# Agent attention ahead of a feed-forward: key scores from two parts (bf16 and fp32r) instead of three, their fp32r products set among the feed-forward's, and the query exchanges made by transfers

## The chip, the core and the metric

The kernel runs on one core of a Trainium2 chip. The metric is the device time of one execution in microseconds; the span of the profile runs from the first to the last instruction of the program. Engines are named as in the profile: PE (TensorE, matmuls), PEld (its weight loads), DVE (VectorE), ACT (ScalarE), POOL (GpSimd) and SP (SyncE, which issues most loads and stores).

## The reference

Four batches of 12480 queries, keys and values of width 128 meet through 49 agents; the result, 49920 tokens of width 128, goes through a feed-forward of width 2048. All inputs are fp32.

```
scale = 1 / sqrt(128)
sm(a, b): softmax over the last axis of scale * (a @ b.T)
agent_v = sm(agents, k) @ v            # per batch, 49 x 128
x       = sm(q, agents) @ agent_v      # per batch, 12480 x 128
h = x.reshape(49920, 128) @ w_in       # 128 x 2048
out = (h * sigmoid(1.702 * h)) @ w_out # 2048 x 128
```

## The kernel before

The product agent_v @ w_in is formed once per batch, so that the first layer of the feed-forward takes the 49 attention weights of a token as its rows. The tokens are cut into 52 groups of 960 (13 per batch). A group is a **turn** of 17 **gaps**; in 16 of them PE does one **unit**, a slice of 128 of the 2048 hidden columns.

A unit on PE is nine pairs of matmuls of 480 columns. `up` makes three pairs into `ph` (high and low f16 parts of weights and attention, each half of the tokens on its own half of the array's rows); `down`, called twice in a gap, makes six pairs into `po` for a unit that is some six gaps older. Both matmuls of a pair use one half of the array's rows each and run side by side. ACT makes the gelu `g` from `ph`; `gh` and `gl`, high and low parts of `g`, are made by ACT or DVE (f16), or by a casting transfer that POOL issues and a subtraction on DVE (fp32r; which units go that way is in `MOVED`).

Between units, `gap(t)` calls the jobs planned for gap t: all the attention work of the later batches. The order of instructions on every engine is the order in which the code is written; nothing is rescheduled. Numbers such as `K_AT`, `MAX_AT`, `SUMS_AT` and `BACK_AT` say in which gap a job stands.

Key scores of the batches 1 to 3: the keys come in 13 groups of 960 per batch. 37 of these 39 groups are scored by `scores`, in two **runs** in neighbouring gaps t and t+1; the first two groups of batch 1 are done in plain fp32 (`scores_exact`). For a group, `split` cuts the fp32 keys `kt` into three bf16 parts. The first is the upper half of each word. DVE makes `rest` as `kt` minus that (line 241) and then the third part from `rest` (line 243), each for one half of the group, so four DVE instructions in the gaps t-4 to t-1. A run then has for each of four blocks of keys four pairs of bf16 products with the agents' parts in `ag_part`: 98, 98, 49 and 49 columns, from `kt`, `rest`, `kt` and `rest`. All 16 pairs of a run stand in one block ahead of the gap's unit.

Where a PSUM bank passes from one half of the array's rows to the other, `half_matmul` lets the new writer wait for a matmul noted by `rest()`, through an instruction on SP's queue (a relay). `rest()` is called at the start of a gap and after `up`.

Queries: scores of two groups lie transposed on DVE with the 49 agents of a token on two blocks of 32 partitions, so the largest value (`query_max`) and the sum (`query_sums`) of each block have to be exchanged with the neighbouring block. `exchange` does that with four copies of 32x30 on DVE (line 680), once for the largest values (`tops`, then `query_shift` at line 693) and once for the sums (then `query_recip` at line 712).

Of the kernel before, what the change touches and what calls it, by code (L numbers as in the profile page):

```python
# [8 lines left out]
F32 = mybir.dt.float32  # L9
# [9 lines left out]
P = 128  # L19
# [14 lines left out]
V_AT = ((0, 6, 12), (4, 11))  # L34
OWN_EXP = (12, 11)
MAX_AT = (21, 23, 25)
SUMS_AT = (3, 5)
BACK_AT = (6, 12)
HIGH_AT = (8, 14)
LOW_AT = (9, 14.5)  # L40
# [21 lines left out]
def kernel(  # L62
# [158 lines left out]
    for i in range(3):  # L221
        nc.vector.tensor_copy(out=ag_part[:, :, i, :], in_=rest)
        if i < 2:
            ag_rest = work.tile([P, B, A], F32, name="ag_rest", tag="o")
            nc.vector.tensor_sub(out=ag_rest, in0=rest, in1=ag_part[:, :, i, :])
            rest = ag_rest

    def halves(t):
        w = t.bitcast(BF16).rearrange("p (n w) -> p n w", w=2)
        return w[:, :, 1], w[:, :, 0]  # L230
# [1 line left out]


    def split(t):
        r = work.tile([P, GT + PAD], F32, name="rest", tag="rest", bufs=1)
        nc.gpsimd.memset(t[:, :PAD], 0.0)

        def piece(i):
            s = slice(0, CH + PAD) if i < 2 else slice(CH + PAD, GT + PAD)
            if i % 2 == 0:  # L240
                nc.vector.tensor_sub(out=r[:, s], in0=t[:, s], in1=halves(t)[0][:, s])
            else:
                nc.vector.tensor_sub(out=halves(r)[1][:, s], in0=r[:, s], in1=halves(r)[0][:, s])  # L243

        return (halves(t)[0], halves(r)[0], halves(r)[1]), piece

    writers = {}
    order = [0, None]
# [33 lines left out]
    def two_banks():  # L282
        return ps_m.tile([P, 2, 512], F32, name="ps_m")

    def scores(b, parts, ps, run, wide):


        x0, x1, x2 = parts
        if wide:
            products = [(x0, 0, 2, 0), (x1, 0, 2, 0), (x0, 2, 1, 0), (x2, 0, 1, 1)]  # L290
        else:
            products = [(x0, 0, 1, 0), (x0, 1, 1, 0), (x0, 2, 1, 0), (x1, 0, 1, 0), (x1, 1, 1, 0), (x2, 0, 1, 0)]
        for j in range(KB // 2):
            for i, (x, y, n, group) in enumerate(products):
                for c in range(2):
                    bank = c ^ run
                    t = (bank * KB // 2 + j) * TB
                    r = slice(c * H, (c + 1) * H)
                    at = (j * 2 + group if wide else j) * A
                    half_matmul(  # L300
                        (ps.name, bank),
                        c,
                        out=ps[:, bank, at : at + n * A],
                        lhsT=x[r, t : t + P],
                        rhs=ag_part[r, b, y : y + n, :].rearrange("p y a -> p (y a)"),
                        start=(run == 0 and i == 0 and j == 0),
                        stop=(run == 1 and i == len(products) - 1 and j == KB // 2 - 1),
                        skip_group_check=True,
                    )

    def scores_exact(b, x, out):

# [8 lines left out]
    def score_banks():  # L321
        ps = two_banks()
        return ps, ps[:, :, : KB // 2 * A].rearrange("p c (j a) -> p c j a", a=A)
# [352 lines left out]
    def exchange(t, x, quarters, by):  # L676

        for i in quarters:
            to = i ^ 1
            by(out=x[to * BL : (to + 1) * BL], in_=t[i * BL : (i + 1) * BL])  # L680

    def query_turn(n, ps):
        if n // 2 not in es:
            es[n // 2] = work.tile([P, 2, CH], F32, name="e")
        nc.vector.transpose(out=es[n // 2][:, n % 2, :], in_=ps[:, :CH])
# [55 lines left out]
    def up(f, wts, pairs, factor):  # L741
        wh, wl = wts
        q_hi, q_lo = pairs
        cols = slice(f * P, (f + 1) * P)
        ph = up_banks()
        products = [(wh, q_hi), (wh, q_lo), (wl, q_hi)]
        for k, (w, q) in enumerate(products):
            for c in range(2):
                r = slice(c * H, c * H + KR)
                half_matmul(  # L750
                    (ph.name, c),
                    c,
                    out=ph[:, c, :CH],
                    lhsT=w[r, cols],
                    rhs=q[r],
                    start=(k == 0),
                    stop=(k == 2),
                )
        g = gpool.tile([P, 2, CH], F32, name="g", bufs=G_BUFS)
        nc.scalar.activation(out=g, in_=ph[:, :, :CH], func=AF.Gelu_apprx_sigmoid, scale=factor)  # L760
        return g
# [53 lines left out]
    def down(u, gh, gl, po, swap, begin, end):  # L815
        products = down_products(u, gh, gl)
        for i, (w, x) in enumerate(products):
            for c in range(2):
                to = c ^ swap
                r = slice(c * H, (c + 1) * H)  # L820
                half_matmul(
                    po[to][0],
                    c,
                    out=po[to][1][:, :CH],
                    lhsT=w[r],
                    rhs=x[r, to, :],
                    start=(begin and i == 0),
                    stop=(end and i == len(products) - 1),
                )

    def down_whole(u, gh, gl, po, end):
        products = [(c, i) for c in range(2) for i in range(3)] if end else [(c, i) for i in range(3) for c in range(2)]
# [75 lines left out]

    def do_key_scores(b, g, c):
        if c == 0:  # L910
            banks[b, g] = wide_banks() if (b, g) in wide else score_banks()
        if (b, g) not in exact:
            scores(b, k_parts[b, g], banks[b, g][0], c, (b, g) in wide)
        elif c == 0:
            scores_exact(b, kts.pop((b, g)), columns(banks[b, g][0]))

# [335 lines left out]
    def plan_queries_of(k, alone):  # L1252
        t = LAG + (2 * k - 3) * GAPS
        d = BEHIND if 2 * k - 3 >= FREE else 0
        if k == 1:
            for at_, q in ((LAG + 3, 2), (LAG + 11, 3)):
                put(at_, lambda q=q: do_query_scores(q))
                put(at_ + 1, lambda q=q: do_query_turn(q))
            before = (LAG + 13, LAG + 14, LAG + 15)
        elif alone:  # L1260
            for i, at_ in enumerate((t - GAPS, t)):
                put(at_ - 12, lambda q=2 * k + i: do_query_load(q))
                put(at_, lambda q=2 * k + i: do_query_scores(q))
                put(at_ + 1, lambda q=2 * k + i: do_query_turn(q))
            before = tuple(t + x for x in MAX_AT)
        else:
            put(t - (12 if k > 2 else 4), lambda: do_query_load(2 * k))
            put(t - (9 if k > 2 else 3), lambda: do_second_load(2 * k + 1))
            put(t + d, lambda: do_query_pair(k))
            for i in range(2):  # L1270
                put(t + d + (0.5, 1)[i], lambda i=i: do_query_turn(2 * k + i))
            before = tuple(t + d + x for x in MAX_AT)
        put(before[0], lambda: do_query_max(k))
        put(before[2], lambda: do_query_shift(k))
        t = LAG + (2 * k - 1) * GAPS
        put(t, lambda: query_exp(k))
        put(t + SUMS_AT[0], lambda: do_query_sums(k))
        put(t + BACK_AT[0], lambda: do_query_recip(k))
        for i in range(2):
            quarters = (2 * i, 2 * i + 1)  # L1280
            put(before[1], lambda q=quarters: do_exchange(k, tops, q, nc.vector.tensor_copy))
            put(t + SUMS_AT[1], lambda q=quarters: do_exchange(k, sums, q, nc.vector.tensor_copy))
            put(t + BACK_AT[i], lambda i=i: do_query_back(k, i))
            put(t + HIGH_AT[i], lambda m=2 * k + i: do_query_high(m))
            put(t + LOW_AT[i], lambda m=2 * k + i: do_query_low(m))
# [171 lines left out]
    def gap(t):  # L1457
        n, k = divmod(t - LAG, GAPS)
        final = n == B * NG - 1
        if t < LAG:  # L1460
            u = t if t < LAG - 1 else None
        elif final:
            u = n * NF + LAG + k
        elif k == 0:
            u = LAG - 1 if n == 0 else None
        else:
            u = n * NF + LAG + k - 1
        before, late[:] = list(late), []
        rest()
        for job in at.pop(t, ()):  # L1470
            job()
        if u is not None:
            if u < total:
                do_up(u)
                rest()
            if k != NF:
                for i in low_of(u, n, k):
                    do_low(i)
        if t >= LAG:
            do_downs(n, k)  # L1480
        if u is not None and k == NF:
            for i in low_of(u, n, k):
                do_low(i)
        for job in at.pop(t + 0.5, ()):
            job()
        for u in before + soon:
            do_high(u)
        soon.clear()
        if k == 2 or final:
            send()  # L1490

    def do_downs(n, k):
# [7 lines left out]
        first_whole = NF - LAG - 1 if n == B * NG - 1 else NF  # L1500
        if 0 < k <= first_whole:
            do_down(n, k - 1, True)
        if k < first_whole:
            do_down(n, k, False)
        elif k < NF:
            do_down_whole(n, k)
        else:
            store(n, po.pop(n))
# [44 lines left out]
```

## Time and profile before

| | |
|---|---|
| median of three runs | 1816.1 us (1814.37 to 1817.16) |
| profiled execution, its own time | 1814.4 us |
| span of its profile | 1812.6 us |
| PE busy | 1772.2 us, 98% |
| DVE busy | 1662.7 us, 92% |
| ACT busy | 1558.2 us, 86% |
| POOL busy | 136.4 us, 8% |

The profiled execution took 1.8 us more than its span. Matmuls are pipelined and their recorded ends overlap, so what PE needs is read from the distance between starts. Idle time of an engine is put down to what released it.

### The profile page before, as it was taken

The numbers are of one execution on the slowest core, as the hardware profiler recorded it, in microseconds if no ns is written. First come the engines' busy times: TensorE is split into PE (matmuls) and PEld (weight loads), VectorE is DVE, ScalarE is ACT, GpSimd is POOL, SyncE is SP. The second block draws the span as 40 slices with busy tenths as digits, with TensorE's granted clock in tenths as the row PEclk, the third lists the DMA queues.
The fourth block names the chain that finished last, engine by engine and source line by source line (L and its number), as shares of the span: only waits on it lengthen the run. The fifth ranks groups of instructions, "written<-read, shape, count | busy, mean of one in ns | idle before, by whom it ended". The sixth has DMA issues, their size and how long they took to land. (4 is left out here: it accounts for less than half of the span.)

```text
span 1812.6 us, 45302 instructions
## 1 busy us (share of the span) xinstructions
PE 1772.2 (98%) x18905; PEld 1099.4 (61%) x18905; DVE 1662.7 (92%) x2337; ACT 1558.2 (86%) x1621; POOL 136.4 (8%) x312
## 2 busy tenths in 40 slices
PE   8899999999999999999999999999999999999999
PEld 8576666677565565566666666566655554555454
DVE  8889998999999999999989999999989889999996
ACT  4677899898878888998888988989878999999997
POOL 0111101111010100101100000011100000000000
PEclk9999999999999999999999999999999999999999
DMA  9565434555442442555443443455421011101000
GB/s 356 184 207 154 157 107 146 171 178 191 135 150 89 152 133 87 182 177 183 170 134 118 130 127 118 136 180 182 167 100 56 23 56 34 47 32 56 13 34 34
DMA packets 78494, 230.41 MB, mean 127 GB/s; under 512 B 8144, under 2 KB 28240, under 8 KB 78288
## 3 DMA queue, kind: packets, MB, share of 16 engines
q1 hardware_dynamic: 43728, 108.25, 19.4%
q0 software_dynamic: 34560, 119.26, 18.5%
q8 instruction: 148, 2.42, 0.6%
q14 instruction: 58, 0.48, 0.1%
HBM read 82.68 MB, written 25.56 MB: 60 GB/s over the span
## 5 line engine op out<-in xcount | busy, mean ns | idle before, releaser
L760 ACT ACTIVATE g<-ph,scales 128x960 f32<-128x960 f32 x832 | 869.5, 1053 | 180.5 <-PE ph L262 173.4
L262 PE MATMUL po<-gh,wo_half 64*128 64x480 f16 x4056 | 738.1, 363 | 6.3 <-DVE o L853 3.8
L262 PE MATMUL ph<-q_hi,wh 56*128 56x480 f16 x3328 | 656.2, 365 | 3.3 <-ACT g L760 3.1
L262 PEld LDWEIGHTS <-wo_half 64*128 64x128 f16 x7236 | 396.2, 94 | 357.8 <-issue 55.9
L801 DVE SCALAR_TENSOR_TENSOR gl<-g,scales,gh 128x960 f16<-128x960 f32 x500 | 592.4, 1208 | 8.0 <-ACT gh L786 6.8
L262 PE MATMUL po<-gl,wo_half 64*128 64x480 f16 x2028 | 411.5, 362 | 4.0 <-DVE gl L801 3.3
L262 PE MATMUL po<-gh,wo 64*128 64x480 f32 x1776 | 415.4, 450 | 0.0
L786 ACT ACTIVATE gh<-g,scales 128x960 f16<-128x960 f32 x361 | 395.6, 1096 | 11.5
L262 PEld LDWEIGHTS <-wh 56*128 56x128 f16 x4992 | 260.9, 94 | 225.5 <-issue 45.4
L262 PE MATMUL ph<-q_lo,wh 56*128 56x480 f16 x1664 | 334.1, 361 | 0.0
L804 DVE TENSOR_TENSOR gl<-g,gh 128x960 fp32r<-128x960 f32 x222 | 253.5, 1148 | 19.0 <-DMA gh<-g 15.6
L262 PEld LDWEIGHTS po<-gh,wo 64*128 64x128 f32 x1776 | 203.6, 185 | 35.5 <-issue 0.6
L792 POOL DMA_DIRECT2D gh<-g x201 | 107.7, 536 | 1501.3 <-ACT g L760 1476.5
L262 PE MATMUL po<-gl,wo 64*128 64x480 f32 x888 | 189.0, 379 | 1.0 <-DVE gl L804 1.0
L801 DVE SCALAR_TENSOR_TENSOR gl<-g,gains,gh 128x960 f16<-128x960 f32 x110 | 131.2, 1207 | 0.2
L262 PE MATMUL ps_m<-gh,wo_half 64*128 64x480 f16 x768 | 128.4, 362 | 0.0
L784 DVE TENSOR_SCALAR gh<-g,scales 128x960 f16<-128x960 f32 x139 | 98.9, 711 | 13.6 <-ACT g L760 13.6
L262 PEld LDWEIGHTS po<-gl,wo 64*128 64x128 f32 x888 | 103.0, 187 | 7.2 <-DVE gl L804 4.5
L786 ACT ACTIVATE gh<-g,gains 128x960 f16<-128x960 f32 x92 | 100.8, 1096 | 3.0
L262 PE MATMUL ps_m<-gl,wo_half 64*128 64x480 f16 x384 | 71.7, 361 | 0.0
L262 PE MATMUL ps_m<-ag_part,rest 64*128 64x49 bf16 (+1 forms) x1184 | 53.4, 192 | 9.4 <-DVE rest L243 9.4
L853 DVE TENSOR_SCALAR o<-po,backs 128x480 f32<-128x480 f32 x62 | 42.6, 714 | 20.6 <-PE po L262 20.0
(206 smaller groups left out, 1419.1 us busy)
## 6 DMA issues: line engine op xcount, KB each, us to landing
gh<-g POOLq DMA_DIRECT2D x201, 480.0 KB, 3.2
vt<-v SPq DMA_DIRECT2D x52, 512.0 KB, 4.2
kt<-kT SPq DMA_DIRECT2D x52, 480.0 KB, 4.2
outT<-o SPq DMA_DIRECT2D x104, 240.0 KB, 2.2
v_pair<-vt POOLq DMA_DIRECT2D x39, 512.0 KB, 3.7
qt<-qT SPq DMA_DIRECT2D x36, 480.0 KB, 3.8
e<-qT SPq DMA_DIRECT2D x14, 480.0 KB, 3.5
words<-w_in SPq DMA_DIRECT2D x4, 512.0 KB, 7.7
```

The source lines that it names most:

```text
L262: ins = nc.tensor.matmul(tile_position=(c * H, 0), **kw)
L760: nc.scalar.activation(out=g, in_=ph[:, :, :CH], func=AF.Gelu_apprx_sigmoid, scale=factor)
L784: nc.vector.tensor_scalar_mul(out=gh, in0=g, scalar1=by)
L786: nc.scalar.mul(out=gh, in_=g, mul=by)
L792: nc.gpsimd.dma_start(out=gh, in_=g)
L801: nc.vector.scalar_tensor_tensor(out=gl, in0=g, scalar=by, in1=gh, op0=ALU.mult, op1=ALU.subtract)
L804: nc.vector.tensor_sub(out=gl, in0=g, in1=gh.bitcast(F32))
L853: nc.vector.tensor_scalar_mul(out=o, in0=po[c][1][:, :CH], scalar1=back)
```

## The change

Keys are in two parts. The bf16 part is as before. The second is the whole remainder, written by one DVE subtraction per half group into a tile of type fp32r (now line 245, in the gaps t-3 and t-1). `ag_near` holds the agents in fp32r with a 50th column of zeros. A run keeps per block the two bf16 pairs from `kt` (98 and 49 columns); the two bf16 pairs from `rest` give way to one fp32r pair of 50 columns. This pair is not written there: it is put into the list `between`, and `fill()` takes one out after each pair of `up` and of `down`. `rest()` is called once more, behind the first `down` of a gap. In the diff, the two lines `fill()` stand at the end of the loops over pairs of `up` and `down`. `exchange_far` makes the exchanges by four transfers issued by POOL; the largest values of the second pair of groups (k = 1) and both exchanges of the first are still copies on DVE. `SUMS_AT[1]` goes from 5 to 4.

```
-            if i % 2 == 0:
+            if i % 2 == 1:
                 nc.vector.tensor_sub(out=r[:, s], in0=t[:, s], in1=halves(t)[0][:, s])
-            else:
-                nc.vector.tensor_sub(out=halves(r)[1][:, s], in0=r[:, s], in1=halves(r)[0][:, s])
...
-            products = [(x0, 0, 2, 0), (x1, 0, 2, 0), (x0, 2, 1, 0), (x2, 0, 1, 1)]
...
         for j in range(KB // 2):
...
+            step(j, x, 0, 2)
+            step(j, x, 2, 1)
+            between.append(lambda j=j: step(j, r_, None, 1))
+
+    between = []
+
+    def fill():
+        if between:
+            between.pop(0)()
...
+    def exchange_far(t, x):
+
+        exchange(t, x, range(4), nc.gpsimd.dma_start)
...
@@ -756,6 +770,7 @@
+            fill()
@@ -827,6 +842,7 @@
+            fill()
@@ -1278,8 +1294,12 @@
-            put(before[1], lambda q=quarters: do_exchange(k, tops, q, nc.vector.tensor_copy))
-            put(t + SUMS_AT[1], lambda q=quarters: do_exchange(k, sums, q, nc.vector.tensor_copy))
+            if k == 1:
+                put(before[1], lambda q=quarters: do_exchange(k, tops, q, nc.vector.tensor_copy))
+            elif not i:
+                put(before[1], lambda: exchange_far(tops[k], others[k]))
+            if not i:
+                put(t + SUMS_AT[1], lambda: exchange_far(sums[k], others[k]))
@@ -1500,6 +1522,7 @@
             do_down(n, k - 1, True)
+            rest()
```

**PE, a first run of a key group.** Before, the 16 bf16 pairs stand together ahead of the unit's first pair; these are the last two blocks' worth (each instruction of a pair is a row; `rest` is the remainder, `kt` the keys).

```order
L262 LDWEIGHTS kt
L262 MATMUL ps_m<-ag_part,kt 128x98
L262 LDWEIGHTS kt
L262 MATMUL ps_m<-ag_part,kt 128x98
L262 LDWEIGHTS rest
L262 MATMUL ps_m<-ag_part,rest 128x98
L262 LDWEIGHTS rest
L262 MATMUL ps_m<-ag_part,rest 128x98
...
L262 LDWEIGHTS wh
L262 MATMUL ph<-q_hi,wh 128x480
```

The same place in the changed kernel, from the run's last bf16 pair on.

```order
L264 LDWEIGHTS kt
L264 MATMUL ps_m<-ag_part,kt 128x49
L264 LDWEIGHTS wh
L264 MATMUL ph<-q_hi,wh 128x480
L264 LDWEIGHTS wh
L264 MATMUL ph<-q_hi,wh 128x480
L264 MATMUL ps_m<-ag_near,rest 128x50 x2
L264 LDWEIGHTS wh
L264 MATMUL ph<-q_lo,wh 128x480
```

The products from `rest` left the block and stand, one pair each, behind the three pairs of `up` and the first pair of `down`; they load their own weights, so no LDWEIGHTS row stands ahead of them.

**DVE, the pieces of a key group of batch 2** (the group whose first run is read below at 588.9 us). Before:

```order
L801 SCALAR_TENSOR_TENSOR gl<-g,scales,gh 128x960
L241 TENSOR_TENSOR rest<-kt 128x488
L801 SCALAR_TENSOR_TENSOR gl<-g,scales,gh 128x960 x2
L373 TENSOR_TENSOR score<-ps_m,score 128x392
L364 TENSOR_TENSOR run_max<-score,run_max 128x392
L243 TENSOR_TENSOR rest<-rest 128x488
L801 SCALAR_TENSOR_TENSOR gl<-g,scales,gh 128x960
L241 TENSOR_TENSOR rest<-kt 128x480
L801 SCALAR_TENSOR_TENSOR gl<-g,scales,gh 128x960
L243 TENSOR_TENSOR rest<-rest 128x480
```

Now:

```order
L816 SCALAR_TENSOR_TENSOR gl<-g,scales,gh 128x960 x3
L383 TENSOR_TENSOR score<-ps_m,score 128x392
L374 TENSOR_TENSOR run_max<-score,run_max 128x392
L245 TENSOR_TENSOR rest<-kt 128x488
L816 SCALAR_TENSOR_TENSOR gl<-g,scales,gh 128x960 x2
L245 TENSOR_TENSOR rest<-kt 128x480
```

Two of the four pieces are gone; the last one keeps its place.

**POOL, around two exchanges of the changed kernel** (`x<-z` sums, `x<-m` largest values, `gh<-g` and `v_pair<-vt` casting transfers). Before, only the rows that are not `x<-` stood there.

```order
L807 DMA gh<-g 128x960 x3
L690 DMA x<-z 32x30 x4
L807 DMA gh<-g 128x960 x2
L240 MEMSET kt 128x8
L807 DMA gh<-g 128x960
L240 MEMSET kt 128x8
L807 DMA gh<-g 128x960 x2
L240 MEMSET kt 128x8
L690 DMA x<-m 32x30 x4
```

Each exchange is four transfers in a row on POOL's queue, with transfers of `gh` and memsets of `kt` behind it.

## Rows read from the trace of the kernel before

**Rows 1.** The page: busy time by engine, and PE's granted clock in 40 slices.
```profile
PE 1772.2 (98%) x18905; PEld 1099.4 (61%) x18905; DVE 1662.7 (92%) x2337; ACT 1558.2 (86%) x1621; POOL 136.4 (8%) x312
...
PEclk9999999999999999999999999999999999999999
```
**Rows 2.** Waits: waiting engine and line, releaser, us in total, times, longest.
```profile
ACT g L760 <- PE ph L262: 173.4, 248, 2.3
...
PE ps_m L262 <- DVE rest L243: 9.4, 8, 1.7
...
PE po L262 <- DVE gl L801: 3.3, 8, 0.8
```
**Rows 3.** Timeline of PE, one run: start, us, instruction, count.
```profile
579.21 0.22 PE L262 MATMUL ps_m<-ag_part,kt 64*128 64x98 bf16 x2
...
579.35 0.22 PE L262 MATMUL ps_m<-ag_part,kt 64*128 64x98 bf16 x2
...
579.77 0.38 PE L262 MATMUL ph<-q_hi,wh 56*128 56x480 f16 x2
579.97 0.38 PE L262 MATMUL ph<-q_lo,wh 56*128 56x480 f16 x2
```
**Rows 4.** Timeline of PE and PEld, fp32r products of the values.
```profile
307.47 0.38 PE L262 MATMUL po<-gh,wo_half 64*128 64x480 f16 x2
307.47 1.13 PEld L262 LDWEIGHTS ps_m<-v_pair,e_pair 64*128 64x128 f32 x16
307.50 1.32 PE L262 MATMUL ps_m<-v_pair,e_pair 64*128 64x260 f32 x16
308.65 0.33 PEld L262 LDWEIGHTS <-wh 56*128 56x128 f16 x6
308.66 0.39 PE L262 MATMUL ph<-q_hi,wh 56*128 56x480 f16 x2
308.87 0.38 PE L262 MATMUL ph<-q_lo,wh 56*128 56x480 f16 x2
```
**Rows 5.** Timeline of PE, a key group in plain fp32.
```profile
84.71 1.99 PE L314 MATMUL ps_m<-ag_key,kt 128*128 128x49 f32 x16
86.62 0.38 PE L262 MATMUL ph<-q_hi,wh 56*128 56x480 f16 x2
```
**Rows 6.** Groups on DVE: count, busy us, mean ns, idle before.
```profile
L243 DVE TENSOR_TENSOR rest<-rest 128x488 bf16<-128x488 f32 x74 | 52.1, 704 | 0.2
L241 DVE TENSOR_TENSOR rest<-kt 128x488 f32<-128x488 f32 x74 | 48.4, 655 | 5.7 <-issue 5.3 <-POOL kt L236 0.4
...
L680 DVE COPY x<-z 32x30 f32<-32x30 f32 x104 | 18.2, 175 | 1.7
L680 DVE COPY x<-m 32x30 f32<-32x30 f32 x104 | 18.0, 173 | 1.8
```
**Rows 7.** Timeline of PE, a first run that waits.
```profile
589.01 0.18 PE L262 MATMUL ps_m<-ag_part,rest 64*128 64x49 bf16 x1
590.08 0.20 PE L262 MATMUL ps_m<-ag_part,rest 64*128 64x49 bf16 x1 [0.90 <-DVE rest L243]
```
**Rows 8.** Timeline of DVE, the pieces of that run.
```profile
587.63 0.66 DVE L241 TENSOR_TENSOR rest<-kt 128x480 f32<-128x480 f32 x1
588.20 1.22 DVE L801 SCALAR_TENSOR_TENSOR gl<-g,scales,gh 128x960 f16<-128x960 f32 x1
589.33 0.70 DVE L243 TENSOR_TENSOR rest<-rest 128x480 bf16<-128x480 f32 x1
```
**Rows 9.** Timeline of DVE, an exchange of sums in a late turn.
```profile
1729.54 0.26 DVE L706 SCALAR_TENSOR_TENSOR z<-e,odd_agent,z 128x30 f32<-128x30 f32 x1
...
1732.66 0.73 DVE L680 COPY x<-z 32x30 f32<-32x30 f32 x4
...
1734.56 0.18 DVE L712 SCALAR_TENSOR_TENSOR z<-x,z 128x30 f32<-128x30 f32 x1
```
**Rows 10.** The page: POOL's casting transfers, and us from issue to landing.
```profile
L792 POOL DMA_DIRECT2D gh<-g x201 | 107.7, 536 | 1501.3 <-ACT g L760 1476.5
...
gh<-g POOLq DMA_DIRECT2D x201, 480.0 KB, 3.2
...
outT<-o SPq DMA_DIRECT2D x104, 240.0 KB, 2.2
```

More of the change, by code (lines that the diff above doesn't have):

```diff
@@ L36 @@
 MAX_AT = (21, 23, 25)
-SUMS_AT = (3, 5)
+SUMS_AT = (3, 4)
 BACK_AT = (6, 12)
@@ L226 @@
             rest = ag_rest
+    ag_near = const.tile([P, B, A + 1], F32R, name="ag_near")
+    nc.vector.tensor_copy(out=ag_near[:, :, 0:A], in_=ag_raw)
+    nc.vector.tensor_scalar_mul(out=ag_near[:, :, A : A + 1], in0=ag_raw[:, :, 0:1], scalar1=0.0)
     def halves(t):
@@ L234, in split @@
     def split(t):
-        r = work.tile([P, GT + PAD], F32, name="rest", tag="rest", bufs=1)
+        r = work.tile([P, GT + PAD], F32R, name="rest", tag="rest", bufs=1)
         nc.gpsimd.memset(t[:, :PAD], 0.0)
@@ L239, in piece @@
             s = slice(0, CH + PAD) if i < 2 else slice(CH + PAD, GT + PAD)
-            if i % 2 == 0:
+            if i % 2 == 1:
                 nc.vector.tensor_sub(out=r[:, s], in0=t[:, s], in1=halves(t)[0][:, s])
-            else:
-                nc.vector.tensor_sub(out=halves(r)[1][:, s], in0=r[:, s], in1=halves(r)[0][:, s])
-        return (halves(t)[0], halves(r)[0], halves(r)[1]), piece
+        return (halves(t)[0], r), piece
     writers = {}
@@ L283, in two_banks, with scores, step @@
         return ps_m.tile([P, 2, 512], F32, name="ps_m")
-    def scores(b, parts, ps, run, wide):
-        x0, x1, x2 = parts
-        if wide:
-            products = [(x0, 0, 2, 0), (x1, 0, 2, 0), (x0, 2, 1, 0), (x2, 0, 1, 1)]
-        else:
-            products = [(x0, 0, 1, 0), (x0, 1, 1, 0), (x0, 2, 1, 0), (x1, 0, 1, 0), (x1, 1, 1, 0), (x2, 0, 1, 0)]
-        for j in range(KB // 2):
[L294 to L309, printed above, removed]
+    def scores(b, parts, ps, run):
+        x, r_ = parts
+        def step(j, w, y, n):
+            for c in range(2):
+                bank = c ^ run
+                t = (bank * KB // 2 + j) * TB
+                r = slice(c * H, (c + 1) * H)
+                at = j * 2 * A
+                rhs = ag_near[r, b, :] if y is None else ag_part[r, b, y : y + n, :].rearrange("p y a -> p (y a)")
+                half_matmul(
+                    (ps.name, bank),
+                    c,
+                    out=ps[:, bank, at : at + rhs.shape[1]],
+                    lhsT=w[r, t : t + P],
+                    rhs=rhs,
+                    start=(run == 0 and y == 0 and j == 0),
+                    stop=(run == 1 and y is None and j == KB // 2 - 1),
+                    skip_group_check=True,
+                )
+        for j in range(KB // 2):
+            step(j, x, 0, 2)
[5 more added lines that the diff above has]
+            between.pop(0)()
     def scores_exact(b, x, out):
@@ L910, in do_key_scores @@
         if c == 0:
-            banks[b, g] = wide_banks() if (b, g) in wide else score_banks()
+            banks[b, g] = score_banks() if (b, g) in exact else wide_banks()
         if (b, g) not in exact:
-            scores(b, k_parts[b, g], banks[b, g][0], c, (b, g) in wide)
+            scores(b, k_parts[b, g], banks[b, g][0], c)
         elif c == 0:
@@ L1480, in gap @@
             do_downs(n, k)
+        while between:
+            fill()
         if u is not None and k == NF:
```

## The prediction

> **What bounds the kernel now.** I read the page first. PE is busy for 98% of the span at full clock, DVE for 92%, ACT for 86% [rows 1]. Since recorded matmuls overlap, 98% alone proves little, so the waits come next: ACT's largest wait is for PE's `ph`, 173.4 us, while PE itself waits little: its largest single cause is DVE's third key part, 9.4 us in 8 waits, then `gl` with 3.3 us [rows 2]. Last, the timeline shows how tight PE's stream is: pairs of 480 columns start 0.20 us apart [rows 3], which is 480 columns at the higher of PE's two clocks, 2.4 GHz. So PE's stream sets the end. A change is worth what it takes from that stream, plus what it takes from PE's waits. DVE work counts only where PE waits for it.
>
> **The change, part by part.**
>
> *Bf16 pairs removed.* A run's first product starts at 579.21 and the unit's first pair at 579.77: 0.56 us. The four blocks of a run are equal, 0.14 us each [rows 3]. A block has pairs of 98, 98, 49 and 49 columns, and one 98 and one 49 go: half, 0.07 us. 37 groups of two runs are 74 runs of four blocks, 296 blocks: 296 x 0.07 = **-20.7 us**.
>
> *Fp32r pairs added*, 296 of them, 50 columns each, every one between two pairs of 480. No row shows an fp32r product this short. The nearest is the values' product, 260 columns of fp32r on half rows: the f16 pair ahead starts at 307.47 and takes 0.20, so the eight pairs run from 307.67 to 308.66, 0.124 us each; 260/480 of 0.20 is 0.110, so a pair costs 0.014 beyond its columns. The first of these weight loads is recorded at 307.47, together with the f16 pair ahead: it lies under that pair. The f16 loads behind the last fp32r pair, however, are recorded only at 308.65, and the f16 pair there takes 0.21 instead of 0.20: leaving fp32r costs another 0.01 [rows 4]. A lone fp32r pair of 50 columns would thus take 0.021 for its columns, 0.014 and 0.01, about 0.045; I take 0.05, since entering and leaving now come with every pair: **+14.8 us**.
>
> The bounds. From below, columns alone: 0.021, +6.2 us. From above, the plain fp32 scores of 49 columns: 16 records from 84.71 to 86.62, 0.12 us each [rows 5], much longer than 49 columns need; if the short fp32r pair costs a record like that, with the same 0.024 around it, it is 0.143 and the sum +42.3 us. I stay near the lower end because rows 5 have such products back to back, where each load can hide only under a neighbour of 49 columns, while here each stands behind 0.20 us of work as the first one of rows 4 does.
>
> A rule that speaks against this: the Trainium skill ("TensorE: Matmul & The Clock Gate", Part 3, "What overlaps and what doesn't") says that weight loads overlap running matmuls only where the row group differs. Here both halves of the rows are busy with the pair ahead, so by that rule the load would be bare; with the page's load time (Part 2, "LDWEIGHTS", columns over 1.2 GHz, an estimate of 0.107 us for 128 columns) a pair would take about 0.15 us and the sum would be +45 us. The loads recorded at 307.47 under a pair on both halves go against that rule for this kernel; the same page (Part 2, "Step-by-step: what each phase is for") itself also allows a load ahead into a background buffer.
>
> *DVE relieved.* Two of four pieces per group go, and the copies: 100.5 us in 148 pieces, of which half, about 50 us; and 196 of 208 copies of 0.174, 34 us [rows 6]. 84 of 1662.7 us. Where does PE feel it? In the run at 588.9, PE stands from 589.01 to 590.08 for a piece that DVE begins at 589.33 and ends at 590.03 [rows 7, 8]. DVE is late there with work queued ahead, so without two pieces, about 1.3 us, it ends that piece near 588.7. PE also comes to it later: 0.28 us of bf16 pairs and one pair of 0.20 precede the first use, so at about 589.4. The wait is gone. The eight waits hold 9.4 us, the longest 1.7 [rows 2]; 1.3 plus the 0.3 later use cover nearly all: **-9 us** (bounds 0 and -9.4). From the other waits for DVE, `gl` above all with 3.3, I take **-2 us** (bounds 0 and -3.3).
>
> *The exchanges.* 49 of them become 196 transfers on POOL. The nearest price of an issue is 0.536 us and the nearest landing of a transfer without a cast 2.2 us, of one issued by POOL 3.2 [rows 10]; theirs are far larger, so I take 4 x 0.53 + 2.2 = 4.3 us from sum to arrival (bounds: 0.53 + 2.2 = 2.7 if only one issue counts and the others overlap landings; 4 x 0.53 + 3.2 = 5.3). The sums are ready at 1729.80 and used at 1734.56; without the 0.73 of copies the use comes at 1733.83, 4.0 us later [rows 9]. So DVE stands 0.3 us in a late turn. Cover: `gl` is made some two gaps ahead of its use on PE, about 3.6 us at nine pairs of 0.20 a gap, and DVE keeps 84 us of relief. If that cover were gone, 25 x 0.3 = 7.5 us would reach PE; I take **+1 us**. The largest values are exchanged between jobs four gaps apart, and not late. Behind an exchange on POOL stand `gh` transfers, for which DVE's `gl` waits; they lose at most 4 x 0.53 = 2.1 us and 201 of them fill POOL to 6%, so I add **+1 us** for the few that follow at once. POOL goes from 136 to about 240 us busy.
>
> *The rest.* The new `rest()` puts the relay's source three pairs (0.6 us) ahead of the next run, as far as `rest()` at a gap's start lies ahead of `down` now; nothing. `ag_near` is two small DVE instructions at the start, where PE waits for other things: nothing, at most 0.5 us. The clock is full and PE gets no new pause: nothing.
>
> **Sum**: -20.7 + 14.8 - 9 - 2 + 1 + 1 = -15.9 on the profiled 1814.4: 1798.5. The median of the runs lies 1.7 above that execution, so **1800 us**, with its own range 1791 to 1808 from the lower bound of the fp32r pair (-8.6) and from waits that stay.
>
> **The rivals.**
>
> *Slower: the short fp32r pair pays for its load or for several passes.* The place is each of the 296 pairs behind a 480-column pair. For it: rows 5, where 49 columns take 0.12. Against it: rows 4. At 0.143 the sum is -20.7 + 42.3 - 9 = +12.6, 1827 in the profiled execution and about 1829 as a median. It decides from 0.10 us a pair on, where 296 x 0.10 = 29.6 eats both the removed pairs (20.7) and the waits (9); at 0.08 it would still end near 1810. Chance 0.22, most of it above 1816.
>
> *The change does half of what it says: PE's waits stay.* DVE may be late at those eight places because of `gl`, which stays, and the wait moves to the fp32r pair. Then -20.7 + 14.8 + 2 = -3.9: 1812. For it: DVE is at 92%; against: the 1.3 us are more than the 1.07 of rows 7. Chance 0.12.
>
> *The transfers are late.* If they land as late as POOL's casts do, at 5.3 us, DVE stands 1.3 us at each of 25 sums, 32 us; were all of it to reach PE: 1830; with the cover above, less than half: 1805 to 1815. Chance 0.08, a quarter of it beyond 1816.
>
> **How the numbers follow.** Chances: forecast 0.58, load paid 0.22, waits stay 0.12, transfers late 0.08. No change I call within 0.2% (3.6 us) of 1816.1, about what a measurement of this kernel can tell: 1812.5 to 1819.7. Faster: 0.57 + 0.07 + 0.05 = 0.69; slower: 0.16 of the first rival and 0.02 of the last = 0.18; same: 0.13. The range leaves out 0.05 below and about 0.12 above: 1790 to 1825.
>
> **What the profile after would show.** Right: in a run's gap, from the first `kt` product to the unit's first pair 0.28 us, and 0.25 us between pairs of 480 with an fp32r pair between them; DVE's busy time near 1580 us; the wait of `ps_m` for `rest` under 1 us; POOL near 240 us; `x` landing in 2 to 2.5 us. Wrong: 0.30 us or more between those pairs; a new wait of DVE for transfers of `x` above 10 us in total, followed by PE waits for `gl`; relay waits of PE on SP at the second runs.

## The result and the profile after

The changed kernel takes **1791.66 us** (median of four runs, 1790.48 to 1792.49) against 1815.49 (1814.37 to 1817.16) for the kernel before on the same chip: a ratio of 0.9868, 95% interval 0.985 to 0.9885, 24 us less. The forecast was 1800 with a range of 1790 to 1825. The profiled execution took 1790.48, its span is 1788.3; before, 1814.4 and 1812.6.

The page of the profile after, as [rows 1]: busy time by engine, and PE's granted clock.

```profile
PE 1760.3 (98%) x18313; PEld 1122.3 (63%) x18313; DVE 1584.7 (89%) x2069; ACT 1556.1 (87%) x1621; POOL 240.0 (13%) x508
...
PEclk9999999999999999999999999999999999999999
```

DVE lost 78 us, POOL gained 104, PE stays at 98% of a shorter span: the kernel is bound by PE's stream as before. The waits after, as [rows 2] (waiting engine and line, releaser, us in total, times, longest), of PE for key parts and `gl`, and of DVE for the exchanges:

```profile
DVE m L707 <- DMA x<-m: 2.0, 1, 2.0
...
PE po L264 <- DVE gl L816: 2.0, 4, 1.1
...
DVE z L726 <- DMA x<-z: 1.1, 3, 0.5
...
PE ps_m L264 <- DVE rest L245: 0.8, 2, 0.7
```

The wait for the key parts fell from 9.4 us to 0.8, and DVE waits 3.1 us in all for the new transfers. PE's timeline of a first run (start, us, instruction, count), as [rows 3]:

```profile
1097.16 0.38 PE L264 MATMUL po<-gh,wo_half 64*128 64x480 f16 x2
1097.37 0.47 PE L264 MATMUL ps_m<-ag_part,kt 64*128 64x98 bf16 x16
1097.66 0.38 PE L264 MATMUL ph<-q_hi,wh 56*128 56x480 f16 x2
1097.68 0.38 PE L264 MATMUL ps_m<-ag_near,rest 64*128 64x50 f32 x2
1097.89 0.39 PE L264 MATMUL ph<-q_lo,wh 56*128 56x480 f16 x2
1097.93 0.38 PE L264 MATMUL ps_m<-ag_near,rest 64*128 64x50 f32 x2
1098.14 0.39 PE L264 MATMUL ph<-q_hi,wh 56*128 56x480 f16 x2
1098.18 0.38 PE L264 MATMUL ps_m<-ag_near,rest 64*128 64x50 f32 x2
1098.38 0.39 PE L264 MATMUL po<-gh,wo_half 64*128 64x480 f16 x2
1098.42 0.38 PE L264 MATMUL ps_m<-ag_near,rest 64*128 64x50 f32 x2
1098.63 0.39 PE L264 MATMUL po<-gl,wo_half 64*128 64x480 f16 x2
1098.84 0.38 PE L264 MATMUL po<-gh,wo_half 64*128 64x480 f16 x2
```

The run's sixteen matmuls (32 before) stand in 0.29 us (1097.37 to 1097.66) where the 32 took 0.56. From there the starts of the 480-column pairs lie 0.23, 0.25, 0.24 and 0.25 apart while an fp32r pair stands between them, and then 0.21. (An fp32r matmul begins in the record 0.02 to 0.04 after the pair ahead of it and lasts 0.38, because matmuls overlap; only the distance between the starts of the long pairs tells what it costs.) Four fp32r pairs stretch a unit of nine f16 pairs from 1.826 us to 1.997 (medians over the units with and without them), so each costs 0.17 / 4 = **0.043 us**.

That holds where all neighbours are f16, in 43 of the 74 runs. In the other 31, fp32r pairs of 480 columns (f32 in the rows; from units in `MOVED`) follow before the four short ones are used up. Such a place, and the same four long pairs with nothing between them:

```profile
593.64 0.39 PE L264 MATMUL ph<-q_hi,wh 56*128 56x480 f16 x2
593.67 0.37 PE L264 MATMUL ps_m<-ag_near,rest 64*128 64x50 f32 x2
593.88 0.47 PE L264 MATMUL po<-gh,wo 64*128 64x480 f32 x2
594.18 0.20 PE L264 MATMUL ps_m<-ag_near,rest 64*128 64x50 f32 x2
594.21 0.47 PE L264 MATMUL po<-gl,wo 64*128 64x480 f32 x2
594.50 0.39 PE L264 MATMUL po<-gh,wo 64*128 64x480 f32 x2
594.73 0.38 PE L264 MATMUL po<-gh,wo_half 64*128 64x480 f16 x2
...
596.81 0.37 PE L264 MATMUL po<-gh,wo_half 64*128 64x480 f16 x2
596.84 0.56 PE L264 MATMUL po<-gh,wo 64*128 64x480 f32 x2
...
597.67 0.38 PE L264 MATMUL ph<-q_hi,wh 56*128 56x480 f16 x2
```

Four long pairs take 1.09 us with two short ones among them (593.64 to 594.73) and 0.86 without (596.81 to 597.67; medians of all such places 1.093 and 0.861): 0.12 us for each short pair. Over a whole unit, four of them stretch six f16 and three fp32r pairs from 1.89 us to 2.19 (medians), 0.075 each.

POOL's new transfers, as [rows 10], from the DMA issues (KB each, median us from issue to landing); each takes POOL 0.52 us:

```profile
x<-z POOLq DMA_DIRECT2D x100, 3.8 KB, 2.3
x<-m POOLq DMA_DIRECT2D x96, 3.8 KB, 3.0
```

**Where the 24 us came from.** The stream: 74 run blocks, each shorter by 0.275 us, are -20.4; the 296 fp32r pairs are +16.7 (43 runs at 0.171 us, 31 at 0.30); together -3.7. PE's waits: the distances between neighbouring starts, less the usual distance for such a pair, counted where more than 0.1 us is left and from 100 us on, add up to 37.5 us before and 19.7 after, -17.8. The sum, -21.5, stands beside a span that fell by 24.3; which distances are taken as usual moves the count of waits by some 2 us, so most of the gain is waits. By what PE stood before, the waits moved so: key products from `rest` 10.5 to 1.2; `gl` in `down` 8.1 to 2.8; a run's first products from `kt` 2.1 to 0; small products 1.1 to 0.3; `gh` in `down` (10.9 to 10.7) and `ph` (3.5 both times) stayed.

### The profile page after: what moved, and what is told of

Its sections match the earlier page's. It is cut to its first block, busy times and chain, and to the rows that moved or that the text cites. A ratio compares the mean times of both kernels' runs of the same rounds, so it can differ in the third digit from the quotient of the medians.

```text
span 1788.3 us, 44228 instructions
## 1 busy us (share of the span) xinstructions
PE 1760.3 (98%) x18313; PEld 1122.3 (63%) x18313; DVE 1584.7 (89%) x2069; ACT 1556.1 (87%) x1621; POOL 240.0 (13%) x508
## 3 DMA queue, kind: packets, MB, share of 16 engines
q1 hardware_dynamic: 43728, 108.25, 19.5%
## 5 line engine op out<-in xcount | busy, mean ns | idle before, releaser
L816 DVE SCALAR_TENSOR_TENSOR gl<-g,scales,gh 128x960 f16<-128x960 f32 x500 | 592.0, 1209 | 13.0 <-ACT gh L801 12.7
L264 PE MATMUL po<-gl,wo_half 64*128 64x480 f16 x2028 | 417.7, 362 | 2.1 <-DVE gl L816 2.0
L264 PEld LDWEIGHTS <-wh 56*128 56x128 f16 x4992 | 272.7, 94 | 219.7 <-issue 45.1
L264 PE MATMUL ph<-q_lo,wh 56*128 56x480 f16 x1664 | 338.6, 362 | 0.0
L264 PE MATMUL po<-gl,wo 64*128 64x480 f32 x888 | 192.6, 384 | 0.3 <-DVE gl L819 0.3
L799 DVE TENSOR_SCALAR gh<-g,scales 128x960 f16<-128x960 f32 x139 | 99.2, 714 | 16.8 <-ACT g L775 16.8
L690 POOL DMA_DIRECT2D x<-m x96 | 49.4, 521 | 320.9 <-DVE m L703 309.3
L264 PE MATMUL ps_m<-ag_near,rest 64*128 64x50 f32 x592 | 83.0, 341 | 0.8 <-DVE rest L245 0.8
```

The lines of the kernel that those rows point to most:

```text
L264: ins = nc.tensor.matmul(tile_position=(c * H, 0), **kw)
L799: nc.vector.tensor_scalar_mul(out=gh, in0=g, scalar1=by)
L816: nc.vector.scalar_tensor_tensor(out=gl, in0=g, scalar=by, in1=gh, op0=ALU.mult, op1=ALU.subtract)
```

## The experiments

The theory after the result: the gain is the PE stream (the short fp32r pair is cheap because it follows a long pair that covers its load) plus waits of PE that ended because DVE does less. Rivals: the fp32r pair is cheap wherever it stands; the waits ended only because the first use of `rest` comes later; the exchanges by transfer, not the keys, brought the gain.

### The keys alone

The changed kernel with both exchanges as DVE copies again and `SUMS_AT` as before.

```
-            if k == 1:
...
-            elif not i:
-                put(before[1], lambda: exchange_far(tops[k], others[k]))
-            if not i:
-                put(t + SUMS_AT[1], lambda: exchange_far(sums[k], others[k]))
+            put(before[1], lambda q=quarters: do_exchange(k, tops, q, nc.vector.tensor_copy))
+            put(t + SUMS_AT[1], lambda q=quarters: do_exchange(k, sums, q, nc.vector.tensor_copy))
```

> The keys' part of the change alone; all exchanges are copies on DVE again. My theory: PE's stream loses about 7.7 us (20.4 removed, 12.7 added, by the distances between starts), and the waits of PE go mainly because DVE has two pieces fewer per key group. Then 1794 to 1798 us. Rival: the exchanges' 34 us of DVE time are needed for PE's waits to go; then 1801 to 1808 us.

Measured: 1795.38 us (1793.86 to 1797.22), ratio to the kernel before 0.9889 (0.9874 to 0.9904), which ran 1814.9 in that series: -19.5. PE's waits, counted as above, are 22.5 us, of which `rest` 0.5 and `gl` 6.3.

### The exchanges alone

The kernel before with the exchanges by transfer.

```
-SUMS_AT = (3, 5)
+SUMS_AT = (3, 4)
...
+            if k == 1:
+                put(before[1], lambda q=quarters: do_exchange(k, tops, q, nc.vector.tensor_copy))
+            elif not i:
+                put(before[1], lambda: exchange_far(tops[k], others[k]))
+            if not i:
+                put(t + SUMS_AT[1], lambda: exchange_far(sums[k], others[k]))
```

> The exchanges by transfers alone; keys in three bf16 parts as before. My theory: PE's stream is the same, DVE has 34 us less to do, but only 1.5 us of it in two turns, so the eight waits for the third key part shrink by 0.3 to 0.7 us each: 1808 to 1813 us. Rival one: the transfers' lateness and POOL's queue cost PE as much as that: 1814 to 1818. Rival two: the exchanges carry most of the gain in waits: 1803 or less.

Measured: 1808.6 (1806.27 to 1812.31), ratio 0.9964 (0.9951 to 0.9977), -6.3. PE's waits are 29.9 us, with `rest` 6.6 and `gl` 3.9: the relief of DVE by 35 us of copies shortens waits that have nothing to do with queries. The two parts add up: -19.5 - 6.3 = -25.8 against -23.8 for both. The third rival falls for the larger share.

### The fp32r pairs in the run's block

```
-            between.append(lambda j=j: step(j, r_, None, 1))
+            step(j, r_, None, 1)
```

> The changed kernel with each fp32r pair in the block of its run again, behind the bf16 pair of 49 columns of its block of keys, and not behind a pair of the feed-forward. My theory: the fp32r weight load needs about 0.11 us and can hide only under a long pair ahead, so 296 pairs cost 0.11 to 0.13 instead of 0.043 us, and PE needs the last key piece earlier: 1811 to 1818 us. Rival: a lone fp32r pair costs its columns and the exits, 0.043 us, wherever it stands: 1790 to 1795 us.

Measured: 1812.19 (1811.68 to 1814.39), ratio 0.9987 (0.9978 to 0.9997): 20.5 us more than the changed kernel, nearly the whole gain, with PE's waits unchanged (20.2 us). The timeline of PE, a run of this kernel:

```profile
591.07 0.25 PE L264 MATMUL ps_m<-ag_part,kt 64*128 64x98 bf16 x3
591.14 0.27 PE L264 MATMUL ps_m<-ag_near,rest 64*128 64x50 f32 x1
...
591.86 0.43 PE L264 MATMUL ph<-q_hi,wh 56*128 56x480 f16 x2
592.07 0.42 PE L264 MATMUL ph<-q_lo,wh 56*128 56x480 f16 x2
```

The block lasts 0.79 us instead of 0.29 (medians over all runs 0.795 and 0.29): 0.126 us for each fp32r pair, close to the 0.12 of [rows 5], against 0.043 between long f16 pairs. By the blocks the pairs cost 37.4 us here, 20.7 more than the 16.7 of the changed kernel, which is the 20.5 measured. So the instruction itself isn't cheap; its place makes it so. The rival that it is cheap wherever it stands falls. That a long pair ahead covers the load is only part of it: the pairs at 0.12 above have a long pair ahead too, and an fp32r pair behind them. Whether the neighbour ahead or the one behind decides in the block was not separated.

### More fp32r pairs between

The pairs of each run's second and fourth block are made twice, 148 more; their remainders so count twice in the scores.

```
-            between.append(lambda j=j: step(j, r_, None, 1))
+            for _ in range(2 if j % 2 else 1):
+                between.append(lambda j=j: step(j, r_, None, 1))
```

> The changed kernel with the fp32r pairs of the second and fourth block of every run made twice (148 pairs more, each also behind a pair of the feed-forward; these blocks' remainders are counted twice, so the scores differ). It measures the price of a lone fp32r pair. By the distances in the trace after, 0.043 us each: 6.4 us more, 1797 to 1799 us. Rival, part of the price is hidden in waits or in the loads of the neighbours: 0.02 or less, 1792 to 1795; or 0.1 and more, 1806 and up.

Measured: 1798.26 (1797.42 to 1799.32), ratio 0.9911 (0.9896 to 0.9925): 6.6 us more than the changed kernel, 0.045 a pair (0.049 by the spans, 1795.6 and 1788.3; 7.8 us and 0.053 by the ratios, since the kernel before ran 1814.1 in this series). This is a net price. By the distances the 148 pairs take some 10 us: six pairs stretch nine f16 pairs from 1.826 us to 2.083, 0.043 each, but six f16 and three fp32r pairs from 1.89 to 2.33, 0.073 each. Against that PE's waits for `gl` fell from 2.0 us to 0.2, and by the starts those for `gl` and `rest` by some 2. That the whole time gives nearly the 0.043 of one gap is in part luck.

### DVE's work put back

Each half of the remainder is computed twice, so DVE does again what the change took from the keys, and PE's stream stays that of the changed kernel.

```
-            if i % 2 == 1:
-                nc.vector.tensor_sub(out=r[:, s], in0=t[:, s], in1=halves(t)[0][:, s])
+            nc.vector.tensor_sub(out=r[:, s], in0=t[:, s], in1=halves(t)[0][:, s])
```

> The changed kernel, but each half of the remainder is computed twice on DVE, so that DVE has four pieces per key group at their old places again (about 48 us more). My theory, DVE's relief ends PE's waits: they come back in part, since the first use on PE stays some 0.48 us later and the exchanges stay off DVE: 1795 to 1802 us. Rival, the later place of the fp32r pairs alone ends the waits: 1791 to 1793 us.

Measured: 1806.68 (1806.23 to 1807.86), ratio 0.9952 (0.9937 to 0.9967): +15 us for 41.6 us of DVE work, twice the middle of what I expected. PE's waits, counted by starts, rise from 19.7 to 31.5 us, and behind one wait for `rest` the granted clock drops (0.57 from 959 to 963 us), which the changed kernel does not show there; the rows of its waits:

```profile
PE po L263 <- DVE gl L815: 5.5, 9, 1.5
...
PE ps_m L263 <- DVE rest L244: 3.1, 3, 1.7
```

Both kinds come back together (line numbers are one less here). So what ended the waits is that DVE has less in its queue, and `gl` profits as much as `rest`.

### The later use alone

The kernel before, with the two `kt` pairs of all four blocks first in a run and those of the two `rest` parts behind them, which moves the first use of `rest` back by about 0.24 us (from 0.05 to some 0.29 us behind the run's start).

```
-        for j in range(KB // 2):
-            for i, (x, y, n, group) in enumerate(products):
+        for j, i in [(j, i) for part in ((0, 2), (1, 3)) for j in range(KB // 2) for i in part]:
+            for x, y, n, group in products[i : i + 1]:
```

> The kernel before, with the pairs from the keys' upper halves first in each run and those from the remainder behind them, so that PE needs the last key piece 0.2 to 0.28 us later and nothing else changes. If a later use alone ends the waits: the eight waits of about 1.0 to 1.9 us shrink by 0.2 each, 1812 to 1815 us; they go only if DVE is relieved. Rival, the order matters more, since the wait is for the order of the queue: 1806 or less.

Measured: 1813.21 (1811.37 to 1815.08), ratio 0.9988 (0.9979 to 0.9998), with PE's waits at 35.4 us, 2.1 less than before; `rest` still holds 8.3. The second rival falls as the main cause: this shift is worth about 2 us of the 17.8. In the changed kernel the first use stands some 0.2 us later still, behind the first pair of `up`; at the same rate its place would be worth about 4 us, an estimate that no run shows.

### The sums one gap later

The changed kernel with the exchange of the sums written one gap later, where the copies stood.

```
-SUMS_AT = (3, 4)
+SUMS_AT = (3, 5)
```

> The changed kernel with the exchange of sums issued one gap later (SUMS_AT 5), so that the transfers land some 2 us later and DVE has to wait for them at most of the 25 places, 25 to 45 us in total. My theory: gl is made early enough to cover that, PE loses at most 3 us: 1791 to 1795 us. Rival: a wait of DVE for a transfer reaches PE in full: 1805 to 1825 us.

Measured: 1818.09 (1814.32 to 1820.37, ten runs), ratio 1.0014 (1.0004 to 1.0024): **26 us more** than the changed kernel, the whole gain gone. My expectation, that `gl` two gaps ahead would absorb nearly all of it, was wrong, and the rival right. One turn shows why. POOL's timeline there, of the changed kernel and then of this one (this execution is some 13 us later at the same place):

```profile
593.35 0.53 POOL L807 DMA_DIRECT2D gh<-g  x1 [4.57 <-ACT g L775]
594.00 2.00 POOL L690 DMA_DIRECT2D x<-z  x4
596.37 0.57 POOL L807 DMA_DIRECT2D gh<-g  x1 [0.37 <-ACT g L775]
```

```profile
606.48 0.53 POOL L807 DMA_DIRECT2D gh<-g  x1 [4.57 <-ACT g L775]
609.51 0.53 POOL L807 DMA_DIRECT2D gh<-g  x1 [2.50 <-ACT g L775]
610.14 1.99 POOL L690 DMA_DIRECT2D x<-z  x4
```

DVE ends the sums near 593.3 and near 606.4, so both exchanges could start within 0.7 us, behind the first `gh` transfer. The later one stands behind a second `gh` transfer as well, which waits 2.5 us for ACT, and is issued 3.0 us later: 610.14 against 606.48 + 0.65. Then it meets a load of queries and one of keys, issued at 608.84 and 611.13; in the changed kernel these are issued at 595.71 and 597.99, 1.7 us and more behind the exchange. The DMA view of 609 to 618 us in the later kernel (busy share in slices; KB each, median us to landing):

```profile
DMA  1005911998798999998998889999973221110000
...
x<-z POOLq DMA_DIRECT2D x4, 3.8 KB, 4.7
```

It lands after 4.7 us; in the changed kernel the four of this turn took 2.6. That the loads make the difference is argued; no run moved them alone. DVE's timeline of the later kernel, and then PE's:

```profile
616.79 0.19 DVE L726 SCALAR_TENSOR_TENSOR z<-x,z 128x30 f32<-128x30 f32 x1 [3.86 <-DMA x<-z]
...
618.58 1.18 DVE L816 SCALAR_TENSOR_TENSOR gl<-g,scales,gh 128x960 f16<-128x960 f32 x1
```

```profile
615.96 0.39 PE L264 MATMUL po<-gh,wo_half 64*128 64x480 f16 x2
619.80 0.38 PE L264 MATMUL po<-gl,wo_half 64*128 64x480 f16 x2 [3.46 <-DVE gl L816]
...
621.15 0.63 PE L264 MATMUL po<-gh,wo_half 64*128 64x480 f16 x2
621.55 0.63 PE L264 MATMUL po<-gl,wo_half 64*128 64x480 f16 x2
...
623.93 0.38 PE L264 MATMUL ph<-q_lo,wh 56*128 56x480 f16 x2
```

DVE stands 3.86 us for `x`, and the `gl` behind it, which PE wants at 616.16, ends at 619.76: PE loses 3.6 of these 3.86 us. In the next such turn read, near 1101 us, it loses 2.7 of 2.92. In a turn without key work, near 1499 us, DVE waits 1.28 us and PE not at all. And behind PE's pause the granted clock fell; windows of the same kernel (stretch, length, busy time of PE, PEld, DVE, ACT and POOL with counts, then clock, DMA share, GB/s):

```profile
618.00:620.00 2.00, 0.20 (x2) 0.11 (x3) 2.00 (x3) 0.60 (x1) 0.00 (x0) 1.00 0.00 0
620.00:622.00 2.00, 2.00 (x16) 0.93 (x14) 2.00 (x3) 0.58 (x1) 0.00 (x0) 0.62 0.00 0
622.00:624.00 2.00, 2.00 (x14) 1.31 (x12) 2.00 (x3) 1.58 (x2) 0.00 (x0) 0.53 0.00 0
624.00:626.00 2.00, 2.00 (x22) 1.21 (x20) 2.00 (x4) 1.42 (x2) 0.00 (x0) 1.00 0.00 0
```

The pairs of 621.15 and 621.55 start 0.40 us apart instead of 0.20, which is 480 columns at 1.2 GHz; nine such pairs, from 620.41 to 623.93, lose 1.7 us (3.52 less 9 x 0.205) on top of the 3.6. In the whole execution PE's waits for `gl` are 16.8 us against 2.0 in the changed kernel, and the mean granted clock 0.992 against 0.998. The granted clock is 0.57 in each of five windows of 4 us (from 125, 204, 620, 1033 and 1105 us), and from 100 us on the changed kernel has no such place. At 1.7 us each these are 8.5 of the 29.4 us by which the span rose, an estimate, beside 14.8 more for `gl`; the rest was not divided.

### The exchanges on SP's queue

```
-        exchange(t, x, range(4), nc.gpsimd.dma_start)
+        exchange(t, x, range(4), nc.sync.dma_start)
```

> The changed kernel with the exchanges issued on SP's queue instead of POOL's. There the relays stand behind them, on which PE's bank changes wait once a gap. Theory: SP waits for the largest values or the sums wherever DVE is late, the relays behind it come late and PE stands up to a few us at many of the 49 places: 1800 to 1840 us. Rival: DVE has made them by then, and SP's transfers land sooner than POOL's: 1788 to 1792 us.

Measured: 1831.97 (1829.95 to 1834.66), ratio 1.0092 (1.0076 to 1.0109), 40 us more than the changed kernel. PE's waits name the place; line 271 is the relay of `half_matmul` on SP's queue. The last row is SP's own wait, at the exchange:

```profile
PE po L264 <- SPq L271: 31.5, 29, 2.5
PE ps_m L264 <- SPq L271: 4.1, 5, 1.0
...
SPq L690 <- DVE z L720: 21.5, 16, 2.6
```

A transfer that waits for DVE's sums holds up the relays behind it, and PE waits for these: 35.6 us in 34 waits, rows that the changed kernel has not got. The same four transfers on POOL have only `gh` transfers and memsets behind them.

## Why the prediction came out as it did

- *What bounds the kernel.* Right: PE's stream and PE's waits together give 21.5 us where the span fell by 24.3. That DVE's work counts only where PE waits for it was right too, but PE feels more of it than its view of waits says: 41.6 us of DVE work put back cost 15 us.
- *Bf16 pairs removed*, -20.7. Measured -20.4.
- *Fp32r pairs added*, +14.8 at 0.05. Right in size, +16.7, but as a mean of two prices: 0.043 a pair in 43 runs and 0.075 in 31, where the prediction knew one. The choice between the bounds by [rows 4] rather than [rows 5] was the important one, and the block, 0.126, shows that place decides. The reason given for it, a long pair ahead, is not the whole: behind a long pair but ahead of an fp32r pair of 480 columns a short pair costs 0.12, which the prediction did not ask about. The rule weighed against it, in the Trainium skill ("TensorE: Matmul & The Clock Gate", Part 3, "What overlaps and what doesn't"), disagrees with this case between f16 pairs: with both halves of the rows busy in the pair ahead it would leave the load bare, an estimate of about 0.15 us a pair by that page's load time, and the runs show 0.043. In the block, where the neighbours have 49 or 98 columns, 0.126 is near that estimate.
- *DVE relieved*, -9 for `rest` and -2 for `gl`. The mechanism held, the size was low: -17.8 in all. `rest` gave 9.3 as forecast. The mis-sized term is the other waits, bounded at 3.3: `gl` had 8.1 us, not 3.3, and lost 5.3; the runs' starts and small products lost 2.9 more. The mistake is in the reading: I took 3.3 from the waits [rows 2], whose idle time is counted between modelled ends. A wait shorter than the overlap of two records shows no idle time, and a longer one shows too little: in [rows 7] the starts are 1.07 us apart and the row says 0.90.
- *The exchanges*, +1 and +1. On the whole time they are a gain: -3.7 in the changed kernel, -6.3 alone, because 35 us of DVE work go, which the prediction counted under DVE relieved, and DVE waits only 3.1 us for them. The landing I worked with (2.2, bounds to 3.2) was right as a median (2.3 and 3.0). Two parts of the step were wrong all the same. The cover, `gl` two gaps ahead, is hardly there in the turns with key work that were read: the sums one gap later show that PE loses nearly all that DVE loses there; I had read it in a late turn [rows 9]. And I asked only which `gh` transfers stand behind an exchange on POOL, not which stand ahead of it: these set its start. In the changed kernel neither comes to bear, because `SUMS_AT` puts the exchange in front of that second `gh`.
- *The rest* (`rest()`, `ag_near`, clock): no new wait on a relay and the clock at 0.998; nothing, as forecast.
- *The sum.* The terms as listed add up to -14.9, not the -15.9 given, so by them the forecast would have been 1801. The measured 1791.66 lies just inside the range, and not for the reason that the range gave: its lower end stood for a cheaper fp32r pair, and the pairs came out 1.9 dearer than forecast. The waits, which the terms allowed 12.7 at most, gave 17.8. That the number held is in part luck.
- *The rivals.* "Load paid" is what the block shows, 1812; where the pairs stand now it holds in part, in the 31 runs at 0.075. "PE's waits stay" did not happen: they are halved. "Transfers late" did not happen at the chosen gap, but its mechanism is real and dearer than I priced it: 1818 one gap later.
- *Signs named ahead.* 0.28 us for a run's block: 0.29. 0.25 between pairs: 0.23 to 0.25 between f16 pairs; but 0.30 or more, named as a sign of being wrong, does stand between two fp32r pairs (593.88 to 594.21). DVE near 1580: 1584.7. `rest` under 1 us: 0.8. POOL near 240: 240.0. `x` in 2 to 2.5 us: 2.3 for the sums, 3.0 for the largest values, a little above.

## What to carry to other kernels

A short product that carries its own weight load belongs between long ones, not beside its like: the same 296 pairs cost 17 us in one place and 37 in the other. Best here were neighbours with a separate weight load on both sides (0.043 each); ahead of long products that carry their own, a pair cost 0.12. When PE is the bound, count what it loses from the distances between starts, not from the idle column, and ask of every engine that feeds it how far ahead it is in the busiest turn, not in a quiet one. Before a small transfer replaces copies, look at what stands ahead of it and behind it on its queue, and what else loads the DMA engines then: one gap and another queue cost 26 and 40 us here.

## What the runs showed of the hardware that I had not expected

- A pair of fp32r matmuls of 50 columns, load included, costs 0.043 us between f16 pairs of 480 columns, 0.12 where fp32r pairs of 480 columns follow, and 0.126 in a block with bf16 pairs of 98 and 49.
- After PE stood 3.6 us, its first pairs still ran at 0.20 us, then nine pairs at about 0.40 with the granted clock at 0.62 and 0.53 in two stretches of 2 us; then full speed again. This wait of PE cost half as much again.
- Transfers of 3.8 KB landed in 2.6 us at one place and in 4.7 at another, where two 480 KB loads had been issued 1.3 us before and 1.0 us after the first of them; no run moved these loads alone.
